# Divided weights in halves, shared by neighbouring products, 22 of their sums kept undivided, and a new order of 104 products

## The chip, the cores and the metric

One core of a Trainium2 chip runs the kernel. Its engines work through a queue each, in order: TensorE (PE, matmuls; PEld is its loading of weights), VectorE (DVE), ScalarE (ACT) and SyncE (SP, which here only issues transfers, DMAs). The metric is the device time of one execution in microseconds (us); lower is better.

## The reference

Sigmoid attention over 8 sequences of 448 tokens with 12 heads of 64, and on its output, 3584 tokens of 768 numbers, a two-layer network with 2048 hidden numbers. All inputs are float32, apart from the weights, which are float64.

```python
scores = scale * np.matmul(q, k.transpose(0, 1, 3, 2)) - np.log(S)
attn = 1.0 / (1.0 + np.exp(-scores))
x = np.matmul(attn, v)            # to (3584, 768)
h = x @ w_in                      # (768, 2048)
g = h * (1.0 / (1.0 + np.exp(-1.702 * h)))
out = g @ w_out                   # (2048, 768)
```

## The kernel before

**Attention** comes first on PE: all of its matmuls stand ahead of the first product of the network. Meanwhile the float64 weights are turned into 16 float32 pieces of 128x1536 (`decode`); the eight of `w_out` go to memory (`whole`, tiles `f`) and come back as `wf`.

**The two layers** are computed by a scheme in the manner of Strassen's. The tokens fall into two groups (q = 0, 1) of four blocks of 448; for each group and layer (m = 0, 1) there are 26 products instead of 32, so 2 x 2 x 26 = 104. A product is named (q, m, r). Its left operand is a sum of weight pieces (`W_SUMS`; the same value v for both groups), its right operand a sum of blocks of x (m = 0) or of g (m = 1), and sums of products (`H_SUMS`, `O_SUMS`) give h and the output. All these sums are DVE instructions (L784, L1218); results leave PSUM through ACT or DVE (L1184, L1185), or ACT puts a sum into PSUM ahead of a product that adds to it (L1142, L1144).

**Dividing.** Each operand of a product is divided into two numbers of the rounded type float32r: a cast gives the high part, a subtraction the rest. For weights that is `split_piece` (L803 on ACT or L804 on DVE, then L806 on DVE), for x and g it is `pair_of` (L1000/L1001, then L1012). A product is three matmuls for each of 12 pairs of blocks, 36 in all (L829).

**Where divided weights live.** `weights_ring` has two buffers (`raw64`) of 128x3072. The first time that a value (m, v) is wanted it is divided in such a buffer, and the divided piece is saved to memory at once (tile `c`, transfer `c<-w`). Each later time it is loaded (`w<-c`, 1536 KB). Nothing is kept from one product to the next, so product number i uses the buffer that product i - 2 leaves. `BUFS` sets how many buffers a kind has.

**Sums and memory.** Undivided sums lie in 14 slots of 128x1536 and 12 of 128x1792. `Sums.used` puts a value away if its next use is further off than `KEEP_FOR` says, in products: leaves of x, of the weights and spilled g are simply loaded again (`x<-xd`, `wf<-f`, `gl<-g`), others are written once (`kw`, `kx`, `kg`) and reloaded.

**The order.** `SEQUENCE` lists the 104 products by hand. `Plan.run` then steps through all tasks with a table of costs (`ISSUE`, `LANDING`, `PER_KB`, `act`, `dve`, `cast`) and puts each into its engine's queue in the order in which it would begin; where ACT and DVE can both do a task, it chooses. The program's queues are fixed by that.

Of the kernel before, what the change touches and what calls it, by code (L numbers as in the profile page):

```python
# [19 lines left out]
P = 128  # L20
# [9 lines left out]
    pair=2, q0=1, q1=1, q2=1, q3=1, h0=1, h1=1, z=1,  # L30
# [5 lines left out]
AGAIN = ((1, 0), (1, 1))  # L36
# [5 lines left out]
ISSUE, LANDING, PER_KB = 0.43, 2.2, 0.0027  # L42
# [72 lines left out]
class Plan:  # L115
    def __init__(self):
        self.tasks, self.rings, self.early, self.slotted, self.gate = [], {}, [], [], []

# [15 lines left out]
    def either(self, costs, emits, deps=(), uses=()):  # L134
        t = Task(emits, costs, deps)
        for b in dict.fromkeys(uses):
            b.users.append(t)
        self.tasks.append(t)
        return t

    def run(self, streams):
# [89 lines left out]
        while count < len(self.tasks):  # L231
# [36 lines left out]
            if e == "SP":  # L268
                free["SP"] = when + ISSUE
                free["DMA"] = max(free["DMA"], when) + cost * PER_KB  # L270
# [114 lines left out]
def sigmoid_attention_mlp(ctx: ExitStack, tc: tile.TileContext, qk, v, w, out):  # L385
# [415 lines left out]
    def split_piece(node, n, into, b, first=lambda: None):  # L801

        t_hi = on_either((act(n), lambda: nc.scalar.copy(into()[:, 0], node.view())),  # L803
                         (cast(n), lambda: nc.vector.tensor_copy(into()[:, 0], node.view())),  # L804
                         [*node.done], [b, node.b], first)
        t_lo = task("DVE", dve(n), lambda: nc.vector.tensor_tensor(  # L806
            into()[:, 1], node.view(), into()[:, 0].bitcast(F32), op=ALU.subtract), [t_hi], [b, node.b])
# [6 lines left out]
    def weights_ring(name):  # L814
        b = buffer("raw64")

        def first():
            if b.tile is None:
                make(b, "raw64", [P, 2 * PIECE], F32, name)

        return b, lambda: b.tile.bitcast(F32R).rearrange("p (t c) -> p t c", t=2), first
# [3 lines left out]
    def matmuls(ps, ws, x, todo, start, stop):  # L825

        for i, (c, k) in enumerate(todo):
            for j, (a, d) in enumerate(TERMS):
                nc.tensor.matmul(  # L829
                    ps, lhsT=ws[:, a, c * P : (c + 1) * P], rhs=x[:, d, k], start=start and i == 0 and j == 0,  # L830
                    stop=stop and i == len(todo) - 1 and j == 2, skip_group_check=True,
                )
# [13 lines left out]
    class Mlp:  # L846


        def __init__(self, sequence, before):
# [3 lines left out]
            self.w_later = {}  # L853
            self.saved, self.begun = {}, set()
# [8 lines left out]
            self.products_of = [(q, m, r) for q, m, r in sequence if q < 2]  # L863
            for i, (q, m, r) in enumerate(sequence):
                v = W_USES[r]
                if (m, v) not in self.begun:
                    self.begun.add((m, v))
                    self.w[m].need(v, i)
                if q < 2:
                    self.w_later[m, v] = self.w_later.get((m, v), 0) + 1  # L870
                    (self.x, self.g)[m][q].need((X_USES, G_USES)[m][r], i)
            self.begun.clear()
# [5 lines left out]
        def build(self):  # L878
            places = {}
            for now, (q, m, r) in enumerate(self.sequence):  # L880
                for sums in (*self.w, *self.x, *self.g):
                    sums.now = now
                if q == 2:
                    if (m, W_USES[r]) not in self.begun:
                        self.w_later[m, W_USES[r]] += 1
                        self.piece_of(q, m, r)
                    continue
# [75 lines left out]

        def piece_of(self, q, m, r):
            v = W_USES[r]
            self.w_later[m, v] -= 1
            self.begun.add((m, v))
            b, into, first = weights_ring(f"w{m}_{q}_{r}")
            if (m, v) in self.saved:
                t = dma(lambda: into().bitcast(F32), in_dram(m, v), 4 * KB, [self.saved[m, v]], [b], first)  # L970
            else:
                sums = self.w[m]
                node = sums.get(v)
                sums.left[v] -= W_USES.count(v)
                t = split_piece(node, PIECE, into, b, first)
                sums.used(v)
                if self.w_later[m, v]:
                    self.saved[m, v] = dma(in_dram(m, v), lambda: into().bitcast(F32), 4 * KB, [t], [b])
            return t, b, into
# [44 lines left out]
        def products(self, q, m, r, uses, n, parts, sign, onto, deps):  # L1024
# [4 lines left out]
            for i in range(parts):  # L1029
                todo = [(i * NJ + j, j) for j in range(NJ)] if m == 0 else [(c * NJ + i, c) for c in range(4)]  # L1030

                def emit(i=i, todo=todo):
                    if ps.tile is None:
                        make(ps, tag, [P, 4, 512], F32, f"p{m}_{q}_{r}")
                    matmuls(ps.tile[:, i, :T], weights(), xb.tile, todo, not more, True)

                t = task("PE", 3 * len(todo) * 0.2, emit, [t_x, t_w, *edge], [ps, xb, wb])
                self.units.append([t])
                done.append(t)
# [189 lines left out]
    last = {tag: plan.rings[tag][-1].users for tag in ("q0", "q1", "q2", "q3")}  # L1229
    mlp = Mlp(SEQUENCE, {"h0": [*last["q0"], *last["q1"]], "h1": [*last["q2"], *last["q3"]]})  # L1230
# [37 lines left out]
```

## Time and profile before

| | us |
|---|---|
| median of 3 runs | 1087.47 (1086.42 to 1089.45) |
| the profiled execution, device time | 1088.81 |
| its span, first to last instruction | 1087.0 |
| PE busy | 1033.0 (95%) |
| DVE busy | 942.3 (87%) |
| ACT busy | 564.6 (52%) |
| mean granted clock of PE | 0.992 |
| moved by DMA | 353.71 MB, 325 GB/s |

Times are of one profiled execution. "Idle before" in a row is the time for which the engine stood still ahead of those instructions, and the name behind the arrow is what ended it. Buffer numbers are left out of names: `w` is any divided weight piece (or a float64 piece in the attention stage), `p` a product in PSUM, `xp` and `gp` divided operands, `xs`, `gs`, `ws` sums, `h` and `o` sums of products.

### The profile page before, as it was taken

How to read it: one execution, taken by the hardware profiler on the slowest of the kernel's cores; microseconds unless marked ns; L12 is line 12 of the kernel's file. 1: busy time of each engine (PE TensorE's matmuls, PEld its weight loads, DVE VectorE, ACT ScalarE, POOL GpSimd, SP SyncE). 2: the span in 40 equal slices, each digit the busy share in tenths (PEclk: the TensorE clock that was granted, in tenths of full speed). 3: DMA queues.
4: the chain of work that ended last, by engine and by line, in shares of the span. 5: the costliest groups of instructions: out<-in, count | busy, mean ns of one | idle time of the engine just before them, and what ended most of it. 6: DMA issues, size and time to landing. Idle time of an engine off the chain costs nothing.

```text
span 1087.0 us, 13651 instructions
## 1 busy us (share of the span) xinstructions
PE 1033.0 (95%) x5588; PEld 836.8 (77%) x5588; DVE 942.3 (87%) x658; ACT 564.6 (52%) x452; POOL 0.2 (0%) x4
## 2 busy tenths in 40 slices
PE   9999999999999899798999989999999988999998
PEld 5554555557888789697888888889888877988887
DVE  6998899887998898898857987999999978879796
ACT  6888877774555665333533724654533422332243
POOL 0000000000000000000000000000000000000000
PEclk9999999999999999999999999999999999999999
DMA  8999888968898899969888976897977898888897
GB/s 336 378 351 389 317 313 323 332 240 319 357 375 330 298 380 347 348 222 355 299 286 322 368 309 249 320 403 280 345 300 292 319 353 346 337 342 316 300 349 268
DMA packets 57902, 353.71 MB, mean 325 GB/s; under 512 B 6000, under 2 KB 14320, under 8 KB 42480
## 3 DMA queue, kind: packets, MB, share of 16 engines
q1 hardware_dynamic: 57840, 352.84, 86.5%
q8 instruction: 44, 0.72, 0.3%
q14 instruction: 18, 0.15, 0.0%
HBM read 212.66 MB, written 140.15 MB: 325 GB/s over the span
## 4 chain that ended last, share of the span: by engine, by line
PE 65%; DMA 18%; DVE 11%; issue 4%; ACT 2%; SPq 0%; DVEq 0%; ACTq 0%
PE p L829 43%; DMA w<-c 13%; PE av L676 9%; PE sc L645 8%; DMA c<-w 3%; DVE h L1218 2%; DVE w L806 2%; PE sc L661 2%; DVE gp L1012 2%; PE av L689 2%; DVE xp L1012 1%; ACT h L1184 1%; DVE gs L784 1%; DMA kw<-ws 1%; DMA kw<-w 1%
## 5 line engine op out<-in xcount | busy, mean ns | idle before, releaser
L829 PE MATMUL p<-gp,w 128*128 128x448 f32 x1872 | 392.2, 370 | 26.6 <-DMA w<-c 17.4
L829 PE MATMUL p<-xp,w 128*128 128x448 f32 x1872 | 390.5, 369 | 22.9 <-DMA w<-c 13.6
L829 PEld LDWEIGHTS p<-gp,w 128*128 128x128 f32 x1872 | 353.3, 190 | 65.2 <-issue 23.7
L829 PEld LDWEIGHTS p<-xp,w 128*128 128x128 f32 x1872 | 352.1, 189 | 61.2 <-issue 21.4
L631 ACT ACTIVATE a<-sc,bias 128x896 f32<-128x896 f32 x168 | 155.9, 1015 | 46.8 <-PE sc L661 30.9
L1184 ACT COPY h<-p 128x1792 f32<-128x1792 f32 x38 | 62.7, 1657 | 107.3 <-PE p L829 78.2
L676 PE MATMUL av<-a,vraw 128*64 128x448 f32 x576 | 113.5, 543 | 0.0
L1184 ACT COPY o<-p 128x1344 f32<-128x1344 f32 x27 | 34.7, 1284 | 122.6 <-PE p L829 89.8
L645 PEld LDWEIGHTS sc<-qk 64*128 64x128 f32 x846 | 75.8, 184 | 26.5 <-PE sc L661 16.2
L645 PE MATMUL sc<-qk 64*128 64x448 f32 x846 | 94.2, 373 | 0.0
L1218 DVE TENSOR_TENSOR h<-h,p 128x1792 f32<-128x1792 f32 x39 | 77.7, 2018 | 13.2 <-ACT h L1184 9.0
L676 PEld LDWEIGHTS av<-a,vraw 128*64 128x64 f32 x576 | 39.2, 137 | 63.2 <-issue 45.1
L1045 ACT ACTIVATE h<-h 128x1792 f32<-128x1792 f32 x31 | 52.2, 1700 | 15.4 <-DVE h L1218 15.4
L515 DVE TENSOR_TENSOR qk<-qkraw,qk 128x896 fp32r<-128x896 f32 x47 | 50.6, 1088 | 0.6
L1000 ACT CAST gp<-gl 128x1792 fp32r<-128x1792 f32 x16 | 27.1, 1697 | 41.8 <-PE p L829 28.8
L1012 DVE TENSOR_TENSOR gp<-gl,gp 128x1792 fp32r<-128x1792 f32 x19 | 38.4, 2023 | 11.6 <-ACT gp L1000 11.5
L1218 DVE TENSOR_TENSOR h<-p,h 128x1792 f32<-128x1792 f32 x14 | 28.3, 2022 | 23.0 <-ACT h L1184 21.5
L1218 DVE TENSOR_TENSOR o<-o,p 128x1344 f32<-128x1344 f32 x27 | 41.6, 1550 | 5.0 <-PE p L829 5.0
L1012 DVE TENSOR_TENSOR xp<-x,xp 128x1344 fp32r<-128x1344 f32 x26 | 40.4, 1553 | 3.9 <-ACT xp L1000 3.9
L803 ACT CAST w<-ws 128x1536 fp32r<-128x1536 f32 x17 | 25.2, 1480 | 35.5 <-PE p L829 29.6
L1000 ACT CAST xp<-x 128x1344 fp32r<-128x1344 f32 x19 | 25.0, 1318 | 28.5 <-PE p L829 22.1
L806 DVE TENSOR_TENSOR w<-ws,w 128x1536 fp32r<-128x1536 f32 x22 | 38.6, 1753 | 1.2 <-ACT w L803 1.1
(113 smaller groups left out, 927.3 us busy)
## 6 DMA issues: line engine op xcount, KB each, us to landing
w<-c SPq DMA_DIRECT2D x56, 1536.0 KB, 7.7
c<-w SPq DMA_DIRECT2D x48, 1536.0 KB, 6.9
w<-w SPq DMA_DIRECT2D x16, 1536.0 KB, 10.0
qkraw<-qk SPq DMA_DIRECT2D x47, 448.0 KB, 6.7
gl<-g SPq DMA_DIRECT2D x20, 896.0 KB, 8.3
g<-h SPq DMA_DIRECT2D x16, 896.0 KB, 8.8
x<-xd SPq DMA_DIRECT2D x21, 672.0 KB, 8.8
kg<-kg SPq DMA_DIRECT2D x14, 896.0 KB, 8.3
```

The costliest lines, as they stand in the source:

```text
L515: lambda: nc.vector.tensor_tensor(lo(), src(), hi().bitcast(F32), op=ALU.subtract),
L631: nc.scalar.activation(a.tile, ps.tile[:, :, :S], AF.Sigmoid, bias=bias, scale=scale)
L645: nc.tensor.matmul(ps.tile[:, j, :S], lhsT=src[kk][rows, S + c * P : S + (c + 1) * P], rhs=src[qq][rows, :S], start=i == 0, stop=i == len( ...
L676: nc.tensor.matmul(ps.tile[cols, n % 2, :S], lhsT=vr.tile[:, at : at + D], rhs=a.tile[:, j], start=c == 0, stop=False, skip_group_check=True,)
L803: t_hi = on_either((act(n), lambda: nc.scalar.copy(into()[:, 0], node.view())), (cast(n), lambda: nc.vector.tensor_copy(into()[:, 0], node ...
L806: t_lo = task("DVE", dve(n), lambda: nc.vector.tensor_tensor(into()[:, 1], node.view(), into()[:, 0].bitcast(F32), op=ALU.subtract), [t_hi ...
L829: nc.tensor.matmul(ps, lhsT=ws[:, a, c * P : (c + 1) * P], rhs=x[:, d, k], start=start and i == 0 and j == 0, stop=stop and i == len(todo) ...
L1000: t_hi = on_either((act(n), lambda: nc.scalar.copy(part(0)(), node.view())), (cast(n), lambda: nc.vector.tensor_copy(part(0)(), node.view())),
L1012: nc.vector.tensor_tensor(part(1)(), node.view(), part(0)().bitcast(F32), op=ALU.subtract)
L1045: t = task("ACT", act(GB), lambda: nc.scalar.activation(view(), node.view(), AF.Gelu_apprx_sigmoid, scale=float(sign)), [*node.done, *(nod ...
L1184: t = on_either((act(self.n), lambda: nc.scalar.copy(view(), node.view())), (dve(self.n), lambda: nc.vector.tensor_copy(view(), node.view())),
L1218: nc.vector.tensor_tensor(view(), x.view(), y.view(), op=ALU.add if s0 == s else ALU.subtract)
```

## The change

Divided pieces are laid out in two halves, each with its high parts and its rests: half 0 serves the first six blocks of the piece, half 1 the others. The two buffers are now two tiles for the whole program, and each half is a buffer of its own for the order (`raw64` for half 0, `w1` for half 1), so that a load is two transfers of 768 KB; the second layer's products go through their blocks half by half. A product whose weights are still in one of the two buffers uses them as they are. `AGAIN` names 8 values of the first layer and 14 of the second that are never saved divided: their undivided sum is kept like any other, and they are divided for each use. `SEQUENCE` and `KEEP_FOR` have new numbers, and so have some costs of the planner.

In all, 56 products divide their weights (48 before), 31 share them (none before) and 17 load them (56 before); 14 divided pieces are saved (48 before).

```diff
-    pair=2, q0=1, q1=1, q2=1, q3=1, h0=1, h1=1, z=1,
+    pair=2, w1=2, q0=1, q1=1, q2=1, q3=1, h0=1, h1=1, z=1,
...
-AGAIN = ((1, 0), (1, 1))
...
-ISSUE, LANDING, PER_KB = 0.43, 2.2, 0.0027
+ISSUE, LANDING, PER_KB, MM = 0.43, (2.2, 2.5), 0.0027, 0.203
+PIECE_RATE = dict(load=0.0032, save=0.0027)
...
 SEQUENCE = (
-    (0, 0, 12), (0, 0, 18), (0, 0, 8), (0, 0, 17), (0, 0, 6), (0, 0, 9), (0, 0, 24), (0, 0, 25),
...
+    (0, 0, 17), (0, 0, 18), (0, 0, 24), (1, 0, 13), (0, 0, 13), (1, 0, 2), (0, 0, 2), (0, 0, 6),
...
+AGAIN = ((1, 5, 8, 11, 13, 17, 21, 24,), (1, 2, 4, 6, 8, 9, 10, 13, 15, 17, 18, 20, 21, 24,))
...
-    def split_piece(node, n, into, b, first=lambda: None):
+    def split_piece(node, n, into, b, wait):
+        def src():
+            return node.view().rearrange("p (h c) -> p h c", h=2)
-        t_hi = on_either((act(n), lambda: nc.scalar.copy(into()[:, 0], node.view())),
+        t_hi = on_either((act(n), lambda: nc.scalar.copy(into()[:, :, 0], src())),
...
     def in_dram(m, v):
-        return lambda: combined[m][v].rearrange("p (t c) -> p t c", t=2)
+        return lambda: combined[m][v].rearrange("p (h t c) -> p h t c", h=2, t=2)
...
+    def weights_ring():
+        old = plan.rings["raw64"][-2:]
+        a, b = buffer("raw64"), buffer("w1")
+        wait = [t for t in old[0].users] if len(plan.rings["w1"]) <= 2 else []
...
+        def into(part=None):
+            if a.turn not in ring_tiles:
+                make(a, "raw64", [P, 2 * PIECE], F32, f"w_{a.turn}")
+                ring_tiles[a.turn] = a.tile
+            at = ring_tiles[a.turn].bitcast(F32R).rearrange("p (h t c) -> p h t c", h=2, t=2)
+            return at if part is None else at[:, part]
+        return (a, b), into, wait
...
+        def ways(self):
+            ways, made, recent = [], set(), [None, None]
+            self.again = set()
+            for q, m, r in self.sequence:
+                v = W_USES[r]
+                if (m, v) in recent:
+                    ways.append("same")
+                    continue
+                if v in AGAIN[m] or (m, v) not in made:
+                    ways.append("made")
+                    made.add((m, v))
+                else:
+                    ways.append("loaded")
+                    self.again.add((m, v))
+                recent = [recent[1], (m, v)]
+            return ways
...
         def piece_of(self, q, m, r):
+            v, way = W_USES[r], self.way[self.now]
+            if way == "same":
+                return next(got for key, got in self.recent if key == (m, v))
+            b, into, wait = weights_ring()
+            if way == "loaded":
+                t = []
+                for h in range(2):
+                    t.append(dma(lambda h=h: into(h).bitcast(F32), lambda h=h: in_dram(m, v)()[:, h], 2 * KB,
+                                 [self.saved[m, v], *(wait if h else [])], [b[h]]))
+                    t[h].rate = PIECE_RATE["load"]
             else:
                 sums = self.w[m]
                 node = sums.get(v)
-                sums.left[v] -= W_USES.count(v)
+                sums.left[v] -= 1
+                t = [split_piece(node, PIECE, into, b, wait)] * 2
                 sums.used(v)
-                if self.w_later[m, v]:
+                if (m, v) in self.again:
+                    save = dma(in_dram(m, v), lambda: into().bitcast(F32), 4 * KB, t[:1], b)
...
-            for i in range(parts):
-                todo = [(i * NJ + j, j) for j in range(NJ)] if m == 0 else [(c * NJ + i, c) for c in range(4)]
+            if m == 0:
+                units = [(i, i // 2, [(i * NJ + j, j) for j in range(NJ)], True, True) for i in range(parts)]
+            else:
+                units = [(i, h, [(c * NJ + i, c) for c in (2 * h, 2 * h + 1)], h == 0, h == 1) for h in range(2) for i in range(parts)]
```

What this does to the queues shows at two places. The first is PE's queue, at the program's last products; `w1_0_8` and the like are divided weights (before: one tile for each use; now `w_0` and `w_1` throughout), `DMAHW...` among the waits stands for a transfer. Before:

```order
L829 MATMUL p1_0_25_7585<-gp0_10_7565,w1_0_25_7567 128x448 [waits DVE_49,DMAHW4_49,PE_49,Activation_49]
L829 MATMUL p1_0_25_7585<-gp0_10_7565,w1_0_25_7567 128x448 x35
L829 MATMUL p1_0_5_7636<-gp0_23_7617,w1_0_5_7615 128x448 [waits DVE_49,DMAHW6_49,PE_49,Activation_49]
L829 MATMUL p1_0_5_7636<-gp0_23_7617,w1_0_5_7615 128x448 x35
L829 MATMUL p1_0_8_7671<-gp0_29_7666,w1_0_8_7668 128x448 [waits DVE_49,DMAHW1_49,PE_49,Activation_49]
L829 MATMUL p1_0_8_7671<-gp0_29_7666,w1_0_8_7668 128x448 x35
```

PE's queue at the same place now:

```order
L845 MATMUL p1_1_6_7631<-gp1_33_7622,w_1_2493 128x448 [waits DVE_49,PE_49,Activation_49]
L845 MATMUL p1_1_6_7631<-gp1_33_7622,w_1_2493 128x448 x35
L845 MATMUL p1_0_6_7683<-gp0_33_7674,w_1_2493 128x448 [waits DVE_49,Activation_49]
L845 MATMUL p1_0_6_7683<-gp0_33_7674,w_1_2493 128x448 x35
L845 MATMUL p1_1_0_7739<-gp1_42_7715,w_0_2647 128x448 [waits DVE_49,PE_49,Activation_49]
L845 MATMUL p1_1_0_7739<-gp1_42_7715,w_0_2647 128x448 x35
```

Before, each of these products waits for a transfer of its own weights; now none does, and the first two use the same piece.

The second place is SP's queue near the 35th product, where divided weights are loaded in both programs (`w<-c`). Before:

```order
L483 DMA w0_1_0_4510<-c0_9_120 128x3072
L483 DMA g0_5_198<-h0_28_3915 128x1792
L483 DMA w0_1_15_4557<-c0_12_123 128x3072
L483 DMA kg1_10_220<-h1_10_3559 128x1792
L483 DMA w0_1_19_4607<-c0_20_131 128x3072
L483 DMA kg1_12_222<-h1_26_4350 128x1792
L483 DMA w0_1_23_4644<-c0_23_134 128x3072
```

SP's queue at the same place now:

```order
L487 DMA w_1_2493<-c0_2_114 128x1536 x2
L487 DMA w_0_2647<-c0_15_126 128x1536
L487 DMA kw0_10_2_4475<-kw0_10_217 128x1536
L487 DMA kx0_16_1_4477<-kx0_16_229 128x1344
L487 DMA w_0_2647<-c0_15_126 128x1536
L487 DMA kw0_15_1_4524<-kw0_15_218 128x1536
L487 DMA w_1_2493<-c0_22_133 128x1536 x2
L487 DMA kx0_15_1_4571<-kx0_15_219 128x1344
```

Each load is two rows of half the size, and between them stand reloads of undivided sums of weights (`kw`) and of x (`kx`), of which there were none at this place.

More of the change, by code (lines that the diff above doesn't have):

```diff
@@ new lines @@
+    w1={0: 12, 1: 12, 2: 3, 3: 6, 4: 25, 5: 12, 6: 6, 8: 12, 9: 12, 10: 25, 11: 3, 13: 25, 15: 3, 17: 12, 18: 25, 19: 6, 20: 3, 21: 3, 22: 6, 23: 3, 24: 3, 25: 6},
+    x0={0: 12, 1: 3, 2: 6, 3: 3, 4: 3, 5: 25, 7: 3, 8: 25, 9: 3, 10: 12, 12: 6, 13: 6, 14: 12, 15: 6, 16: 12, 17: 3, 20: 3, 23: 25, 24: 3},
+    x1={0: 25, 1: 3, 2: 12, 3: 6, 5: 6, 6: 6, 7: 6, 8: 12, 10: 25, 11: 25, 12: 12, 13: 6, 14: 25, 15: 12, 16: 12, 17: 6, 18: 3, 19: 6, 20: 6, 21: 12, 22: 3, 24: 6, 25: 3},
+    g0={0: 12, 1: 25, 2: 12, 4: 12, 5: 25, 6: 12, 8: 6, 9: 12, 10: 3, 11: 3, 12: 3, 13: 12, 14: 6, 15: 25, 16: 25, 17: 3, 18: 12, 20: 3, 21: 12, 22: 6, 23: 6, 24: 3, 25: 25, 26: 25, 29: 3, 30: 6, 31: 3, 32: 25, 35: 12, 37: 6, 38: 6, 39: 12, 40: 25, 41: 6, 42: 25},
@@ L117, in __init__ @@
         self.tasks, self.rings, self.early, self.slotted, self.gate = [], {}, [], [], []
+        self.landing = LANDING[0]
     def buffer(self, tag):
@@ L135, in either @@
         t = Task(emits, costs, deps)
+        t.landing = self.landing
         for b in dict.fromkeys(uses):
@@ L269, in run @@
                 free["SP"] = when + ISSUE
-                free["DMA"] = max(free["DMA"], when) + cost * PER_KB
+                free["DMA"] = max(free["DMA"], when) + cost * t.rate
                 end = free["DMA"] + t.landing
@@ L799, in tiled @@
         return flat if n == PIECE else lambda: flat().rearrange("p (a b) -> p a b", b=T)
-    def split_piece(node, n, into, b, first=lambda: None):
-        t_hi = on_either((act(n), lambda: nc.scalar.copy(into()[:, 0], node.view())),
-                         (cast(n), lambda: nc.vector.tensor_copy(into()[:, 0], node.view())),
-                         [*node.done], [b, node.b], first)
+    def split_piece(node, n, into, b, wait):
+        def src():
+            return node.view().rearrange("p (h c) -> p h c", h=2)
+        t_hi = on_either((act(n), lambda: nc.scalar.copy(into()[:, :, 0], src())),
+                         (cast(n), lambda: nc.vector.tensor_copy(into()[:, :, 0], src())),
+                         [*node.done, *wait], [*b, node.b])
         t_lo = task("DVE", dve(n), lambda: nc.vector.tensor_tensor(
-            into()[:, 1], node.view(), into()[:, 0].bitcast(F32), op=ALU.subtract), [t_hi], [b, node.b])
+            into()[:, :, 1], src(), into()[:, :, 0].bitcast(F32), op=ALU.subtract), [t_hi], [*b, node.b])
         node.readers += [t_hi, t_lo]
@@ L811, in in_dram @@
     def in_dram(m, v):
-        return lambda: combined[m][v].rearrange("p (t c) -> p t c", t=2)
[L814 to L821, printed above, removed]
+        return lambda: combined[m][v].rearrange("p (h t c) -> p h t c", h=2, t=2)
+    ring_tiles = {}
+    def weights_ring():
+        old = plan.rings["raw64"][-2:]
+        a, b = buffer("raw64"), buffer("w1")
+        wait = [t for t in old[0].users] if len(plan.rings["w1"]) <= 2 else []
+        half = PIECE // 2
+        def into(part=None):
[5 more added lines that the diff above has]
+        return (a, b), into, wait
     gate = plan.gate
@@ L829, in matmuls @@
                 nc.tensor.matmul(
-                    ps, lhsT=ws[:, a, c * P : (c + 1) * P], rhs=x[:, d, k], start=start and i == 0 and j == 0,
+                    ps, lhsT=ws(c // 6)[:, a, c % 6 * P : (c % 6 + 1) * P], rhs=x[:, d, k], start=start and i == 0 and j == 0,
                     stop=stop and i == len(todo) - 1 and j == 2, skip_group_check=True,
@@ L852, in __init__ @@
                            KEEP_FOR[f"w{m}"], self.put_w(m)) for m in range(2)]
-            self.w_later = {}
-            self.saved, self.begun = {}, set()
+            self.saved, self.recent = {}, [(None, None)]
+            self.way = self.ways()
             self.x = [Sums(X_SUMS[0], X_USES, self.x_leaf(q), dve(XB), combine, fresh(f"xs{q}", XB, "s"),
@@ L863, in __init__ @@
             self.products_of = [(q, m, r) for q, m, r in sequence if q < 2]
+            for m in range(2):
+                for v in W_USES:
+                    self.w[m].left[v] -= 1
             for i, (q, m, r) in enumerate(sequence):
[L865 to L868, printed above, removed]
+                if self.way[i] == "made":
+                    self.w[m].left[W_USES[r]] += 1
+                    self.w[m].need(W_USES[r], i)
                 if q < 2:
-                    self.w_later[m, v] = self.w_later.get((m, v), 0) + 1
                     (self.x, self.g)[m][q].need((X_USES, G_USES)[m][r], i)
-            self.begun.clear()
             for q in range(2):
@@ L882, in build @@
                     sums.now = now
+                self.now = now
                 if q == 2:
-                    if (m, W_USES[r]) not in self.begun:
-                        self.w_later[m, W_USES[r]] += 1
-                        self.piece_of(q, m, r)
+                    self.piece_of(q, m, r)
                     continue
@@ L962, in put_g @@
             return put
-        def piece_of(self, q, m, r):
[L965 to L970, printed above, removed]
+        def ways(self):
[14 more added lines that the diff above has]
+            return ways
+        def piece_of(self, q, m, r):
+            v, way = W_USES[r], self.way[self.now]
[8 more added lines that the diff above has]
+                    t[h].rate = PIECE_RATE["load"]
             else:
@@ L973, in piece_of @@
                 node = sums.get(v)
-                sums.left[v] -= W_USES.count(v)
-                t = split_piece(node, PIECE, into, b, first)
+                sums.left[v] -= 1
+                t = [split_piece(node, PIECE, into, b, wait)] * 2
                 sums.used(v)
-                if self.w_later[m, v]:
-                    self.saved[m, v] = dma(in_dram(m, v), lambda: into().bitcast(F32), 4 * KB, [t], [b])
+                if (m, v) in self.again:
+                    save = dma(in_dram(m, v), lambda: into().bitcast(F32), 4 * KB, t[:1], b)
+                    save.rate = PIECE_RATE["save"]
+                    self.saved[m, v] = save
+            self.recent = [self.recent[-1], ((m, v), (t, b, into))]
             return t, b, into
@@ L1028, in products, with emit @@
             edge = [*(self.before[tag] if len(plan.rings[tag]) == 1 else []), *deps]
-            for i in range(parts):
-                todo = [(i * NJ + j, j) for j in range(NJ)] if m == 0 else [(c * NJ + i, c) for c in range(4)]
-                def emit(i=i, todo=todo):
+            if m == 0:
+                units = [(i, i // 2, [(i * NJ + j, j) for j in range(NJ)], True, True) for i in range(parts)]
+            else:
+                units = [(i, h, [(c * NJ + i, c) for c in (2 * h, 2 * h + 1)], h == 0, h == 1) for h in range(2) for i in range(parts)]
+            for i, h, todo, first, last in units:
+                def emit(i=i, todo=todo, first=first, last=last):
                     if ps.tile is None:
                         make(ps, tag, [P, 4, 512], F32, f"p{m}_{q}_{r}")
-                    matmuls(ps.tile[:, i, :T], weights(), xb.tile, todo, not more, True)
-                t = task("PE", 3 * len(todo) * 0.2, emit, [t_x, t_w, *edge], [ps, xb, wb])
+                    matmuls(ps.tile[:, i, :T], weights, xb.tile, todo, first and not more, last)
+                t = task("PE", 3 * len(todo) * MM, emit, [t_x, t_w[h], *edge], [ps, xb, wb[h]])
                 self.units.append([t])
-                done.append(t)
+                if last:
+                    done.append(t)
             return done
@@ L1229, in sigmoid_attention_mlp @@
     last = {tag: plan.rings[tag][-1].users for tag in ("q0", "q1", "q2", "q3")}
+    plan.landing = LANDING[1]
     mlp = Mlp(SEQUENCE, {"h0": [*last["q0"], *last["q1"]], "h1": [*last["q2"], *last["q3"]]})
```

10 lines of the change are left out of this document (3 added, 7 removed), and 24 rows, old and new, of the table SEQUENCE.

## The prediction

> **What bounds the kernel now.** The page's totals come first, then the chain that ended last: the work of TensorE (PE) and waits for transfers make up most of it.
>
> ```profile
> span 1087.0 us, 13651 instructions
> PE 1033.0 (95%) x5588; PEld 836.8 (77%) x5588; DVE 942.3 (87%) x658; ACT 564.6 (52%) x452; POOL 0.2 (0%) x4
> PE 65%; DMA 18%; DVE 11%; issue 4%; ACT 2%; SPq 0%; DVEq 0%; ACTq 0%
> PE p L829 43%; DMA w<-c 13%; PE av L676 9%; PE sc L645 8%; DMA c<-w 3%; DVE h L1218 2%; DVE w L806 2%; PE sc L661 2%; DVE gp L1012 2%; PE av L689 2%; DVE xp L1012 1%; ACT h L1184 1%; DVE gs L784 1%; DMA kw<-ws 1%; DMA kw<-w 1%
> ```
>
> The order of instructions puts all of attention on PE ahead of the first product, so the second view is the windows of the two stages (columns: window, its length, busy us of PE, PEld, DVE, ACT, POOL with instructions, granted clock, DMA share, GB/s).
>
> ```profile
> 0.00:252.50 252.50, 251.10 (x1844) 131.45 (x1845) 217.84 (x226) 199.07 (x203) 0.20 (x4) 1.00 0.89 328
> 252.50:1084.00 831.50, 781.86 (x3744) 705.31 (x3744) 724.43 (x432) 365.39 (x250) 0.00 (x0) 0.99 0.87 326
> ```
>
> Attention leaves PE 1.4 us idle, and PE's order there does not change: I keep its 252.5 us. The stage of the 104 products takes 831.1 us, to the end of the last matmul below (1083.6). PE idles 49.5 us in it (26.6 + 22.9 in the page's two groups of products); the view of PE's waits in this stage says for what, and PE's timeline shows places.
>
> ```profile
> PE p L829 <- DMA w<-c: 31.0, 21, 4.7
> PE p L829 <- DVE gp L1012: 6.1, 6, 1.6
> PE p L829 <- DVE xp L1012: 5.1, 7, 1.5
> PE p L829 <- DVE w L806: 2.4, 2, 1.3
> ```
>
> ```profile
> 252.51 14.83 PE L829 MATMUL p<-xp,w 128*128 128x448 f32 x72 [0.23 <-DVE xp L1012]
> 370.50 8.06 PE L829 MATMUL p<-xp,w 128*128 128x448 f32 x37 [0.38 <-DMA w<-c]
> 453.01 38.28 PE L829 MATMUL p<-xp,w 128*128 128x448 f32 x180 [4.44 <-DMA w<-c]
> 558.22 30.97 PE L829 MATMUL p<-xp,w 128*128 128x448 f32 x144 [2.12 <-DMA w<-c]
> 716.02 59.34 PE L829 MATMUL p<-gp,w 128*128 128x448 f32 x288 [1.06 <-DVE gp L1012]
> ```
>
> And the end of the timeline of all engines:
>
> ```profile
> 1066.97 0.32 SPq L483 DMA_DIRECT2D w<-c  x1
> 1069.92 2.02 DVE L1012 TENSOR_TENSOR gp<-gl,gp 128x1792 fp32r<-128x1792 f32 x1
> 1075.92 7.67 PE L829 MATMUL p<-gp,w 128*128 128x448 f32 x36 [1.54 <-DMA w<-c]
> ```
>
> Three readings. One product is 36 matmuls, and eight in a row without a wait took 59.34 us: 7.42 us each. Second, 31.0 of the 49.5 idle us, in 21 waits, are for divided weights that come back from memory. The last three rows show how: the load is issued at 1066.97, when the product before the last ended and freed its buffer; only one product lies between, and the load lands 8.9 us later, 1.54 us after that product is done. Third, nothing else was late there: the other operand was ready at 1069.92 + 2.02 = 1071.94, four microseconds before. So this time is PE's to win, until VectorE (DVE), 87% busy in the stage, is late in its turn.
>
> A fourth reading is the clock (third column from the end):
>
> ```profile
> 450.00:500.00 50.00, 46.44 (x220) 42.41 (x221) 42.37 (x29) 17.74 (x13) 0.00 (x0) 0.97 0.77 281
> 900.00:950.00 50.00, 46.48 (x218) 42.05 (x219) 44.30 (x27) 15.77 (x11) 0.00 (x0) 0.97 0.89 351
> ```
>
> ```profile
> 453.00:456.00 3.00, 2.99 (x8) 2.69 (x9) 3.00 (x3) 0.99 (x1) 0.00 (x0) 0.52 1.05 442
> 509.40:512.00 2.60, 2.56 (x13) 2.42 (x14) 2.10 (x2) 0.49 (x1) 0.00 (x0) 1.00 1.07 378
> 558.20:561.00 2.80, 2.78 (x9) 2.55 (x10) 0.39 (x1) 0.00 (x0) 0.00 (x0) 0.63 1.02 345
> ```
>
> Cut into stretches of 50 us, the stage has five at 0.97 (the first and the last are shown) and the rest at 1.00. In each a wait for weights is followed by some 3 us at about half clock, as at 453 and 558. 0.03 x 50 x 5 = 7.5 us go there, counted as busy. Check of the model: 104 x 7.42 + 49.5 + 7.5 = 828.7 of 831.1; the 2.4 left are ends of broken stretches.
>
> **The change, part by part.** The transfers and the groups of instructions give the prices (mean or median in each row).
>
> ```profile
> w<-c SPq DMA_DIRECT2D x56, 1536.0 KB, 7.7
> c<-w SPq DMA_DIRECT2D x48, 1536.0 KB, 6.9
> gl<-g SPq DMA_DIRECT2D x20, 896.0 KB, 8.3
> x<-xd SPq DMA_DIRECT2D x21, 672.0 KB, 8.8
> kg<-kg SPq DMA_DIRECT2D x14, 896.0 KB, 8.3
> kw<-kw SPq DMA_DIRECT2D x11, 768.0 KB, 8.2
> wf<-f SPq DMA_DIRECT2D x11, 768.0 KB, 11.7
> kx<-kx SPq DMA_DIRECT2D x5, 672.0 KB, 9.3
> ```
>
> ```profile
> L806 DVE TENSOR_TENSOR w<-ws,w 128x1536 fp32r<-128x1536 f32 x22 | 38.6, 1753 | 1.2 <-ACT w L803 1.1
> L803 ACT CAST w<-ws 128x1536 fp32r<-128x1536 f32 x17 | 25.2, 1480 | 35.5 <-PE p L829 29.6 <-DVE ws L784 3.3 <-DMA c<-w 2.6
> L804 DVE CAST w<-ws 128x1536 fp32r<-128x1536 f32 x5 | 4.8, 958 | 0.2 <-DMA c<-w 0.2
> L1218 DVE TENSOR_TENSOR o<-o,p 128x1344 f32<-128x1344 f32 x27 | 41.6, 1550 | 5.0 <-PE p L829 5.0
> L1185 DVE COPY o<-p 128x1344 f32<-128x1344 f32 x7 | 10.9, 1556 | 10.2 <-ACT o L1184 5.7 <-PE p L829 4.3
> L1184 ACT COPY o<-p 128x1344 f32<-128x1344 f32 x27 | 34.7, 1284 | 122.6 <-PE p L829 89.8 <-DVE o L1218 14.4 <-DMA out<-o 10.4
> ```
>
> DVE's waits for transfers in the stage, the two longest of three:
>
> ```profile
> DVE xs L784 <- DMA kw<-w: 4.9, 1, 4.9
> DVE x L784 <- DMA x<-xd: 0.5, 1, 0.5
> ```
>
> *Weights.* Of the 104 products 56 now divide their weights afresh (48 before), 31 use those of a neighbour, and 17 load (56 before). So the wait that cost 31.0 us meets 17 loads instead of 56. Each is two halves, and a half is issued when the product two weights earlier has finished with that half: half a product, 3.7 us, more head start, 11.1 us against the 7.7 of a whole load. Bounds: 0 if that hides all, 17 x 31.0/56 = 9.4 if a load waits as long as now. I take 2, near the hidden end, since 8.9 us (the example above) fits into 11.1. The matmuls are as many in both programs; those of the second layer now run half by half, at no cost I can see.
>
> *Clock.* The dips follow the long waits, so four of five should go: 6.0 us, between 0 and 7.5. The Trainium skill, "TensorE: Matmul & The Clock Gate", Part 1, says that the array falls to half clock after at least one idle window of about 3.4 us. This trace agrees only in part: 0.63 was granted after a gap of 2.12 us. By the page only the gaps over 3.4 us, the 4.44 us at 453 and one of 4.7, would matter, two of the five, and the sum would come out 3.0 us higher.
>
> *Dividing on ACT and DVE.* Eight more divisions: 8 x 1.753 on DVE and five more casts on ACT (5 x 1.48 = 7.4), three on DVE (2.9). The pieces are now written as 2 x 768 with a stride; no row shows a DVE cast of that form. Between 0.958 and the slow pass of 1.753, 12 casts, that is 0 to 9.5 us of DVE; I take 0, since the runs of 768 are still contiguous. Counting all other instructions of both orders, DVE loses 8 sums of 1344 (12.4) and 8 copies out of PSUM (12.9), and gains 0.8 in small ones: 16.9 - 12.4 - 12.9 + 0.8 = -7.6 us. ACT gains 13 copies of 1344 (16.7), loses 8 of 1792, and fills PSUM ahead of 40 products instead of 28 (about 15): some 25 us, on an engine that is busy for 365 of 831 us; nothing of it is on the path.
>
> *How evenly DVE is loaded.* I add up DVE's instructions between the starts of products, by their rows. The work exceeds 7.42 us a product by 9 us over the worst run before (21 products, which hold the 59.34 us without a wait), by 7 us over the worst run now (one product). So the waits that aren't for weights should stay what they are: 49.5 - 31.0 = 18.5 us, DVE's for the most part. A faster PE leaves less slack, a smaller DVE load gives some back; I leave it at 18.5.
>
> *Transfers.* 39 loads and 34 saves of 1536 KB go (-114.8 MB). To free memory the new table sends sums away sooner: 147 reloads of x, g and w operands instead of 82, and 51 writes instead of 26 (+71.7 MB). In all -43 MB of the stage's 271 (326 GB/s x 831.5 us), which at 800 us is 285 GB/s. DVE waited for transfers of such operands hardly more than 5 us in this stage before, at its very start. I cost the 65 added reloads at nothing; the cover is that they are issued products ahead. If it goes, each is a trip of 8 to 12 us. The queue of SyncE issues some thirty more transfers at 0.32 us, 10 us over 800.
>
> *The end* stays: 1087.0 - 1083.6 = 3.4 us.
>
> **Sum:** 252.5 + 104 x 7.42 (771.7) + 18.5 + 2 + 1.5 (one dip) + 1.5 (ends of stretches) + 3.4 = 1051.1 us of span. The profiled execution took 1088.81 for its 1087.0, and the median of the runs, 1087.47, is 1.3 below it: 1051.1 + 1.8 - 1.3 = 1051.6. I say 1051.
>
> **Rivals.** *DVE is the bound.* From 252.51 to 370.1 nothing waited for weights, and 15 products still took 117.6 us, 7.84 each, with small waits for DVE. If that is the pace everywhere: 252.5 + 815.4 + 3.4 + 0.5 = 1072. For it: DVE would be busy for 717 of 800 us. Against it: the 59.34 us.
>
> *Everything hides.* The DVE waits shrink too: 252.5 + 771.7 + about 8 + 3.4 + 0.5 = 1036. The smaller, evener DVE load speaks for it, the waits of 1.0 to 1.6 us for DVE all over the stage against it.
>
> *Late reloads, slower than before.* DVE takes its queue in order; if a reload isn't there, every later sum and division waits, and PE runs dry. Four or five lost trips of 8.3 us eat the 36 us; from there on it is slower, and eight give about 1051 + 66 = 1117. The 65 added reloads, and their place on one SyncE queue behind loads that wait for PE, speak for it; against it speak 5 us of such waits in 82 reloads, and a lower DMA load.
>
> *No change:* DVE is late by as much wherever weights were late, 1087. The four microseconds of slack in the rows at 1069.92 speak against it.
>
> **Chances and range.** My forecast (1040 to 1064) 0.62, DVE's pace (1064 to 1078) 0.15, everything hides (1030 to 1040) 0.10, no change 0.05, late reloads 0.08. The range from 1034 to 1077 leaves out the last two, and the ends of the two before. A measurement of this kernel tells 0.3% from no change: faster 0.87, same 0.05, slower 0.08.
>
> **What would show it.** Right: PE's waits for `w<-c` at a few us; product stretches of 7.42 each; no stretch at half clock after the start; DVE busy above 89% of the stage; the first product still near 252.5. Wrong: a row of DVE waiting for `kg`, `kw`, `kx`, `x` or `wf` with more than 15 us in total (late reloads), PE waiting for `w` or `gp` divisions for over 35 us (DVE's pace), casts of 2x768 at 1.7 us, or a long wait at the first product of the second layer, which now stands 27th instead of 45th.

## The result, and the profile after

| | before | after |
|---|---|---|
| median | 1086.95 us | 1042.84 us (1038.97 to 1045.04) |
| profiled execution, device time | 1088.81 us | 1043.49 us |
| its span | 1087.0 us | 1041.7 us |
| PE idle in the products' stage | 49.5 us | 11.7 us |
| moved by DMA | 353.71 MB | 310.63 MB |

The ratio is 0.9587, with a 95% interval of 0.9554 to 0.9621: 4.1% faster. The forecast was 1051 us, range 1034 to 1077.

The page of the changed kernel: totals, and the chain that ended last.

```profile
span 1041.7 us, 13721 instructions
PE 1024.7 (98%) x5588; PEld 832.3 (80%) x5588; DVE 933.7 (90%) x654; ACT 588.4 (56%) x473; POOL 0.2 (0%) x4
PE 34%; DVE 3%; issue 0%; DMA 0%; ACT 0%; DVEq 0%; ACTq 0%
PE p L845 34%; DVE gp L1052 1%; DVE o L1262 1%; DVE w L813 0%; DVE kg L788 0%; DMA wf<-f 0%; DVE h L1262 0%; DVE wf L788 0%; ACT p L1186 0%; DVE xp L1052 0%; ACT o L1228 0%; DVE gp L1041 0%; ACT o L1116 0%; DVEq L788 0%; ACTq L1186 0%
```

This chain is followed back only to 640 us, so its shares cannot be set beside those of before; from there on it is almost only matmuls, and `w<-c`, 13% of the chain before, is not in it. The two stages (columns as before), PE's waits in the second, and four rows of PE's timeline:

```profile
0.00:253.00 253.00, 251.15 (x1840) 131.42 (x1844) 217.23 (x225) 201.41 (x204) 0.20 (x4) 1.00 0.90 334
253.00:1040.00 787.00, 773.56 (x3752) 700.84 (x3744) 716.52 (x429) 387.03 (x269) 0.00 (x0) 1.00 0.76 287
```

```profile
PE p L845 <- DVE xp L1052: 7.5, 10, 1.7
PE p L845 <- ACT p L1186: 1.9, 2, 1.5
PE p L845 <- DVE w L813: 1.1, 1, 1.1
PE p L845 <- PE p L845: 0.6, 1, 0.6
PE p L845 <- DVE gp L1052: 0.2, 1, 0.2
PE p L845 <- DVE xp L1054: 0.2, 1, 0.2
```

```profile
253.67 14.86 PE L845 MATMUL p<-xp,w 128*128 128x448 f32 x72
650.98 22.14 PE L845 MATMUL p<-xp,w 128*128 128x448 f32 x108 [1.46 <-ACT p L1186]
672.96 320.38 PE L845 MATMUL p<-gp,w 128*128 128x448 f32 x1548
993.56 44.76 PE L845 MATMUL p<-gp,w 128*128 128x448 f32 x216 [0.22 <-DVE gp L1052]
```

No wait for a weight load is left, the granted clock is 1.00 in both stages, and from 672.96 on 43 products run without a gap: 320.38 / 43 = 7.45 us each. Nearly all that PE still waits for is VectorE or ScalarE, mostly in the first layer. The transfers that correspond to those of before:

```profile
w<-c SPq DMA_DIRECT2D x34, 768.0 KB, 5.8
kg<-kg SPq DMA_DIRECT2D x27, 896.0 KB, 7.4
gl<-g SPq DMA_DIRECT2D x26, 896.0 KB, 7.4
x<-xd SPq DMA_DIRECT2D x34, 672.0 KB, 7.4
c<-w SPq DMA_DIRECT2D x14, 1536.0 KB, 8.0
kw<-kw SPq DMA_DIRECT2D x25, 768.0 KB, 7.4
```

The reloads became more and land sooner (7.4 us where they took 8.2 to 8.8), at 287 GB/s instead of 326; the 14 saves `c<-w` land later (8.0 us instead of 6.9).

### The profile page after: what moved, and what is told of

The parts are those of the page before. It is cut to its first block, busy times and chain, and to the rows that moved or that the text cites. A ratio compares the mean times of both kernels' runs of the same rounds, so it can differ in the third digit from the quotient of the medians.

```text
span 1041.7 us, 13721 instructions
## 1 busy us (share of the span) xinstructions
PE 1024.7 (98%) x5588; PEld 832.3 (80%) x5588; DVE 933.7 (90%) x654; ACT 588.4 (56%) x473; POOL 0.2 (0%) x4
## 2 busy tenths in 40 slices
DMA packets 62799, 310.63 MB, mean 298 GB/s; under 512 B 6544, under 2 KB 14864, under 8 KB 58896
## 5 line engine op out<-in xcount | busy, mean ns | idle before, releaser
L1228 ACT COPY h<-p 128x1792 f32<-128x1792 f32 x30 | 49.7, 1657 | 106.7 <-PE p L845 65.0
L1228 ACT COPY o<-p 128x1344 f32<-128x1344 f32 x37 | 47.1, 1283 | 101.8 <-PE p L845 95.5
L1262 DVE TENSOR_TENSOR o<-o,p 128x1344 f32<-128x1344 f32 x34 | 52.2, 1549 | 7.5 <-ACT o L1228 5.1
L1089 ACT ACTIVATE h<-h 128x1792 f32<-128x1792 f32 x28 | 47.5, 1702 | 14.5 <-DVE h L1262 14.5
L710 DVE COPY x<-av 128x896 f32<-128x896 f32 x23 | 25.1, 1089 | 18.6 <-PE av L693 18.6
L1052 DVE TENSOR_TENSOR gp<-gs,gp 128x1792 fp32r<-128x1792 f32 x19 | 38.4, 2022 | 2.6 <-ACT gp L1040 2.2
L1052 DVE TENSOR_TENSOR gp<-kg,gp 128x1792 fp32r<-128x1792 f32 x18 | 36.3, 2019 | 1.7 <-ACT gp L1040 1.5
L813 DVE TENSOR_TENSOR w<-ws,w 128x1536 fp32r<-128x1536 f32 x19 | 33.3, 1752 | 1.3 <-ACT w L810 1.1
L514 DVE CAST qk<-qkraw 128x896 fp32r<-128x896 f32 x37 | 22.8, 622 | 12.4 <-DMA qkraw<-qk 6.1
L813 DVE TENSOR_TENSOR w<-kw,w 128x1536 fp32r<-128x1536 f32 x18 | 31.5, 1752 | 2.6 <-ACT w L810 2.6
```

What stands on the lines that cost most here:

```text
L514: (costs[1], lambda: nc.vector.tensor_copy(hi(), src())),
L710: (1.09, lambda: nc.vector.tensor_copy(xb.tile, ps.tile[:, :, :S])), [t], [xb, ps], rows)
L813: t_lo = task("DVE", dve(n), lambda: nc.vector.tensor_tensor(into()[:, :, 1], src(), into()[:, :, 0].bitcast(F32), op=ALU.subtract), [t_hi ...
L1052: nc.vector.tensor_tensor(part(1)(), node.view(), part(0)().bitcast(F32), op=ALU.subtract)
L1089: t = task("ACT", act(GB), lambda: nc.scalar.activation(view(), node.view(), AF.Gelu_apprx_sigmoid, scale=float(sign)), [*node.done, *(nod ...
L1228: t = on_either((act(self.n), lambda: nc.scalar.copy(view(), node.view())), (dve(self.n), lambda: nc.vector.tensor_copy(view(), node.view())),
```

## The experiments

Every kernel here is ordered anew by the planner inside it, so an edit also moves instructions that it doesn't name. How much that alone can do is the last group's question. "PE idle" is that of the products' stage, from the view of PE's waits. Each ratio is to runs of the kernel before that were made beside it, whose medians lie between 1086.95 and 1088.86.

| | median us | ratio to before (95%) | PE idle | of it weight loads | DMA MB |
|---|---|---|---|---|---|
| before | 1086.95 | 1 | 49 | 31.0 | 353.71 |
| after | 1042.84 | 0.9587 (0.9554 to 0.9621) | 11.5 | 0 | 310.63 |
| 1 old order, halves | 1092.09 | 1.0034 (1.0016 to 1.0052) | 49 | 1.9 | 347.43 |
| 2 old order, whole loads | 1102.37 | 1.0124 (1.0102 to 1.0146) | 55 | 21.1 | 347.41 |
| 3 new order, nothing shared | 1211.93 | 1.1121 (1.1093 to 1.1149) | 141 | 126.5 | 420.73 |
| 4 after, whole loads | 1055.41 | 0.9689 (0.9669 to 0.971) | 22 | 11.1 | 310.62 |
| 5 as 1, old costs | 1100.15 | 1.0125 (1.0093 to 1.0157) | 54 | 1.5 | 347.43 |
| 6 as 1, own queue | 1093.09 | 1.0059 (1.004 to 1.0078) | 50 | 9.0 | 347.43 |
| 7 after, no sum kept | 1056.70 | 0.9731 (0.9697 to 0.9766) | 23 | 0 | 331.07 |
| 8 after, old costs | 1054.36 | 0.9698 (0.9657 to 0.974) | 23 | 0 | 310.63 |
| 9 after, divided for each | 1098.76 | 1.0116 (1.0087 to 1.0145) | 56 | 0 | 315.34 |
| 10 after, saves back | 1103.66 | 1.0151 (1.0135 to 1.0167) | 61 | 3.5 | 376.69 |
| 11 after, casts on ACT | 1051.37 | 0.9668 (0.9652 to 0.9685) | 21 | 0 | 310.63 |
| 12 after, matmul cost | 1049.51 | 0.9654 (0.9639 to 0.9668) | 18 | 1.0 | 310.63 |

**Are the weight loads the whole story?** Experiment 1 takes the waits for them away and keeps the old order.

```diff
 SEQUENCE = (
-    (0, 0, 17), (0, 0, 18), (0, 0, 24), (1, 0, 13), (0, 0, 13), (1, 0, 2), (0, 0, 2), (0, 0, 6),
+    (0, 0, 12), (0, 0, 18), (0, 0, 8), (0, 0, 17), (0, 0, 6), (0, 0, 9), (0, 0, 24), (0, 0, 25),
...
-AGAIN = ((1, 5, 8, 11, 13, 17, 21, 24,), (1, 2, 4, 6, 8, 9, 10, 13, 15, 17, 18, 20, 21, 24,))
+AGAIN = ((), ())
```

(`KEEP_FOR` as before, too.)

> The changed kernel with the old order of products, the old table of what is put away, and no sum kept undivided: 54 of 104 products load their weights, in halves, 2 share. Theory 1 (what was won is the lateness of divided weights; a head start is enough): each load gets 3.7 us of head start, of the 31.0 us of waits for weights only what exceeds 3.7 us stays (two waits, about 2 us), and the half-clock dips go: 1087 - 29 - 7 = about 1051. Theory 2 (the new order with its evener VectorE work wins the time): the order is the old one, so 1080 to 1087. Rival 3 (transfers are limited by bandwidth, with the same bytes as before): loads land as late as now, 1080 or more.

PE's waits in the products' stage (us in total, times, longest):

```profile
PE p L845 <- issue: 13.2, 4, 6.8
PE p L845 <- DVE gp L1052: 9.2, 7, 2.3
PE p L845 <- DVE xp L1052: 8.5, 10, 1.4
PE p L845 <- DVE w L813: 5.9, 5, 1.3
PE p L845 <- ACT h L1228: 3.7, 1, 3.7
...
PE p L845 <- DMA w<-c: 1.9, 2, 1.5
```

Half of theory 1 holds: in halves, the waits for loads fall from 31.0 to 1.9 us, as expected. The other half falls: nothing is won, 1092, above theory 2's range too, and rival 3's late loads are not in the rows. As much idle time is there as before, 49 us, under other names. The longest of the waits called "issue" shows whose they are (timeline of the same run):

```profile
789.90 3.98 PE L845 MATMUL p<-gp,w 128*128 128x448 f32 x18 [0.42 <-DMA w<-c]
794.64 2.03 DVE L788 TENSOR_TENSOR h<-h,gs 128x1792 f32<-128x1792 f32 x1
796.76 1.68 ACT L1040 CAST gp<-h 128x1792 fp32r<-128x1792 f32 x1 [1.57 <-DVE h L788]
798.52 2.02 DVE L1052 TENSOR_TENSOR gp<-h,gp 128x1792 fp32r<-128x1792 f32 x1
800.64 5.57 PE L845 MATMUL p<-gp,w 128*128 128x448 f32 x18 [6.77 <-issue]
```

PE is done at 793.9; the last sum for its next operand starts at 794.64 and the division ends at 800.54, a tenth of a microsecond before PE goes on. By the timeline DVE has had no break since 785.8; it came to this operand only now. In the kernel before, the same operand was ready hardly earlier, at 800.31:

```profile
798.28 2.03 DVE L1012 TENSOR_TENSOR gp<-h,gp 128x1792 fp32r<-128x1792 f32 x1
```

There PE had waited 2.63 us for weights at 794.39 and went on from that product to this one without a gap. At this place the weights' lateness had covered the lateness of the operand. The last product, on which the prediction's third reading rests, is another case. Its operand was ready at 1071.94 in the kernel before and is ready at 1076.98 here:

```profile
1074.95 2.03 DVE L1052 TENSOR_TENSOR gp<-gl,gp 128x1792 fp32r<-128x1792 f32 x1
1077.07 3.46 PE L845 MATMUL p<-gp,w 128*128 128x448 f32 x9 [3.43 <-issue]
```

Two sums of g now stand close ahead of its division in DVE's queue (from 1068.37 and 1071.77), and PE waits 3.43 us for it. So a part of the new idle time comes from the planner's new placing; how much, these runs do not say.

Experiment 2 undoes the halves in that kernel: one transfer, `[self.saved[m, v], *wait], b)` for both halves.

> As the first, but each load is one transfer of 1536 KB, which waits until both halves of the buffer are free: the kernel before, with the new cost table of the planner and two products that share. Theory 1: about 1085, with waits for weights of about 30 us. Theory 2: the same. If the planner's costs alone had won the time, about 1045.

1102, where I had expected about 1085. It is 10 us slower than the first, with 21.1 us of waits for loads. So in the old order halves take 19 us of waits away and are worth 10 us, but 1102 is 15 us above the kernel before, from which it differs by the planner's costs, the layout in halves and two shared products. Experiment 5 puts the costs back with halves:

```diff
-ISSUE, LANDING, PER_KB, MM = 0.43, (2.2, 2.5), 0.0027, 0.203
-PIECE_RATE = dict(load=0.0032, save=0.0027)
+ISSUE, LANDING, PER_KB, MM = 0.43, (2.2, 2.2), 0.0027, 0.2
+PIECE_RATE = dict(load=0.0027, save=0.0027)
```

> As the first experiment (old order, loads in halves, no sum kept), but with the planner's old costs, so that only the halves and two shared products differ from the kernel before. Theory 1 (a head start for the weights is enough; in the first experiment the new costs spoiled an order that was tuned with the old ones): 1055. Theory 4, from the first experiment (in the old order VectorE's divisions and reloads are late right behind the weights, whatever the costs): waits for weights of 2 us again, but 1075 to 1090.

1100, slower than both expectations, again with hardly a wait for loads (1.5 us). So nothing shows that the new costs held experiment 1 back. The next suspect is SyncE's queue, on which reloads stand behind loads that wait for PE; experiment 6 issues the loads from GpSimd's queue (`nc.gpsimd.dma_start` for `w<-c` alone):

> As the first experiment, but the loads of divided weights are issued from GpSimd's queue instead of SyncE's. Theory 4a (in the old order the reloads of operands stand behind weight loads that wait for PE on SyncE's queue, and this head-of-line wait makes VectorE late): the waits for divisions shrink, about 1060. Theory 4b (the order itself, the distance between a sum and its use, makes VectorE late): 1085 to 1095, as the first.

1093, as the first: theory 4a finds no support. It is not refuted either, since this queue is no like for like: GpSimd is then 58.6 us busy with issuing, and 9.0 us of waits for loads come back.

**What the new order needs.** Experiment 3 gives the kernel before the new `SEQUENCE` and `KEEP_FOR` and nothing else.

> The kernel before with the new order and the new table of what is put away: 48 products divide and save, 56 load whole pieces, none share. Theory 1: a neighbour now loads what was saved a product before; a save (6.9 us) and a load (7.7 us) in a row against 7.4 us of cover cost some 4 us for about 27 such pairs, so slower than before: 1130 to 1200, with all of it in waits for weights. Theory 2 (the order as such wins): 1050 to 1065.

The longest of PE's waits:

```profile
PE p L829 <- DMA w<-c: 126.5, 33, 9.1
```

1212: a neighbour that can't share has to wait for a save and a load. There are 33 such waits at 3.8 us, where I had expected some 27 at 4; the time lies above the expected 1130 to 1200. PE idles 92 us more than before, and the rest of the 125 us goes with a lower granted clock (0.946 instead of 0.992). The new order does not pay without sharing. Experiment 4 takes the halves from the changed kernel's 17 loads, with the same edit as experiment 2:

> The changed kernel with its 17 loads in one transfer each instead of two halves. Theory 1 as predicted (17 loads that cost 31.0/56 us each if they are as late as before): up to 9 us of waits for weights come back and a dip or two, 1045 to 1056. Rival: sharing and few loads hide them without halves: 1043, no wait for weights.

The two longest of PE's waits:

```profile
PE p L845 <- DMA w<-c: 11.1, 6, 4.0
PE p L845 <- DVE xp L1049: 7.5, 9, 1.6
```

The 12.6 us that it loses are nearly all in one row: 11.1 us in six waits for whole loads, while the waits for xp stay where they were (7.5). In this order, what halves win arrives in the time.

Experiment 9 keeps the order and lets nobody share, dividing the 31 pieces again:

```diff
-                if (m, v) in recent:
-                    ways.append("same")
-                    continue
-                if v in AGAIN[m] or (m, v) not in made:
+                if (m, v) in recent or v in AGAIN[m] or (m, v) not in made:
```

> The changed kernel in which no product uses a neighbour's weights: the 31 shared pieces are divided again for each product (87 divisions, 17 loads, same order of products). VectorE gets 31 x 1.753 = 54 us more and is wanted for about 771 of the 785 us that the products' stage takes. Theory 4b (VectorE is what the order has to keep ahead; sharing spares it): 1070 to 1100, with the loss in waits for divisions of w, xp and gp. If VectorE's load leaves room: 1045 to 1055.

The four longest of PE's waits:

```profile
PE p L845 <- DVE gp L1049: 22.4, 17, 2.9
PE p L845 <- ACT p L1183: 11.5, 3, 10.3
PE p L845 <- DVE xp L1049: 9.2, 8, 2.1
PE p L845 <- DVE w L813: 7.9, 9, 1.3
```

The stage's window in the same run (DVE is the fifth number):

```profile
253.00:1100.00 847.00, 790.36 (x3748) 711.63 (x3744) 772.98 (x465) 423.92 (x296) 0.00 (x0) 0.98 0.73 272
```

1099, within theory 4b's 1070 to 1100. DVE now works 773 us in the stage, 56 more, and most of what PE waits for is divisions. That the time grows by 56 as well is partly chance: 10.3 us are one wait for ScalarE to fill PSUM, at the product where experiments 8 and 11 below lose as much, and the granted clock is 0.98. Sharing is what leaves DVE the room in which the weights' waits can be cashed in.

Experiment 7 keeps no sum undivided (`AGAIN = ((), ())`), with the new order and sharing.

> The changed kernel with no value kept as an undivided sum: 48 divisions, 24 or 25 loads in halves, 31 shared, 22 pieces saved. Its memory traffic for saves and loads of divided pieces grows by some 8 of each. Theory 1: the loads are hidden by halves and sharing, so the kept sums are worth little: 1043 to 1050. Rival (the kept sums are what frees the time): 1060 or more, with waits for weights.

1057: between the two expectations. There is no wait for loads, as theory 1 has it; the 12 us of added idle time are waits for divisions. Keeping the sums comes out as 14 us here, and the last group shows that placing alone can make 7 to 12 us.

**The transfers.** Experiment 10 saves every divided piece again (`if True:` for `if (m, v) in self.again:`), 42 writes that nobody reads.

> The changed kernel that also saves each of the 56 freshly divided pieces to memory; nothing more reads them (42 writes of 1536 KB, 66 MB, so about as much traffic as the kernel before). Rival 3 (the smaller traffic wins the time): 1065 or more, with later loads and reloads. Theories 1 and 4: the buffer is also held until the save has read it, but neighbours share, so little: 1043 to 1052.

The two longest of PE's waits, and the stage's window:

```profile
PE p L845 <- DVE gp L1052: 22.7, 11, 4.3
PE p L845 <- ACT h L1228: 18.1, 1, 18.1
```

```profile
253.00:1100.00 847.00, 785.13 (x3744) 710.95 (x3744) 726.57 (x438) 374.87 (x260) 0.00 (x0) 0.97 0.89 342
```

1104, all of the gain and more. I had expected 1043 to 1052; the rival's 1065 or more is right, though at 377 MB this kernel moves 23 MB more than the one before. Reloads land later (`x` after 9.4 us and `kg` after 8.7, where both took 7.4). But PE waits for hardly any transfer itself (3.5 us), and DVE's waits for transfers in the stage are 6.0 us, where they were 4.7 (ACT's 13.4, where they were 1.7). One wait of 18.1 us for a copy out of PSUM and many for gp make up the most. Behind the 18.1 us the timeline shows no transfer: the copy stands on ACT behind a gelu, which waits for a sum on DVE, and DVE works without a break from 513.1 to 528.5:

```profile
526.45 2.02 DVE L1262 TENSOR_TENSOR h<-h,h 128x1792 f32<-128x1792 f32 x1
528.50 1.70 ACT L1089 ACTIVATE h<-h 128x1792 f32<-128x1792 f32 x1 [10.77 <-DVE h L1262]
530.11 3.19 ACT L1228 COPY h<-p 128x1792 f32<-128x1792 f32 x2
```

The planner counts these writes too, and places the rest around them. At this place it is the order of work on ACT and DVE; whether the chip's transfers or the planner's placing does the rest, these runs don't separate.

**How much is placing?** Three small edits of the changed kernel: the old costs (8, the diff of experiment 5), all 56 weight casts on ACT (11), and `MM` 0.206 for 0.203 (12).

> The changed kernel with the planner's old costs (landing, rate, matmul); the list of products is the same, so instructions only move a few places in their queues. If the order of products does the work: 1040 to 1050. If the fit between the list and the planner's costs does it: 1055 or more, with the loss in waits for VectorE's divisions.

> The changed kernel with every weight cast on ScalarE (56 instead of 44), 12 x 0.96 = 11.5 us less for VectorE and 12 x 1.48 more for ScalarE, which is half idle. If VectorE's load sets the remaining 12 us of PE waits: 1036 to 1041. If their places in the queues do: 1040 to 1050.

> The changed kernel with the planner's cost of a matmul at 0.206 us, which is what the trace has for long stretches (320.38 us for 1548), instead of 0.203; instructions move a few places. If the fit of the planner's costs to the chip matters most: 1036 to 1041. If the list was fitted to the costs as they are: 1045 to 1055.

All three are slower than the changed kernel, by 7 to 12 us. Experiment 12 is in its second range; 8 lies between its two, and its loss is not in divisions but in one wait for ScalarE. Experiment 11 is slower than both expectations: DVE has only 2 us less work (714 us in the stage instead of 717) where 11.5 were expected, since the planner gave it other tasks. In 8 and 11 it is one place (PE's timelines):

```profile
658.52 24.98 PE L845 MATMUL p<-xp,w 128*128 128x448 f32 x108 [10.35 <-ACT p L1186]
```

```profile
659.48 24.64 PE L843 MATMUL p<-xp,w 128*128 128x448 f32 x108 [10.07 <-ACT p L1184]
```

In the changed kernel the same three products start at 650.98 after a wait of 1.46 us for the same instruction, ScalarE filling PSUM ahead of them. In experiment 8 the timeline has it on ACT behind gelus and copies that take turns with sums and copies on DVE, each waiting for the other's last. So differences of about 10 us between two placings of one list say nothing on the edit, unless a row shows them, as in experiment 4.

## Why the prediction was right, point by point

- *The sum.* Forecast 1051.1 us of span, measured 1041.7. The stage before took 253.7 instead of 252.5; 104 products at 7.42 with ends of stretches 773.2, measured 784.65 - 11.7 = 773.0; the end 3.4, as said. Small changes of the planner's costs move this kernel by 7 to 12 us, so an agreement within 9.4 us is partly luck.
- *Weight loads:* 2 us, measured 0. Experiment 4 shows the halves as the cause: with whole loads 11.1 us come back, a little above the bound of 9.4. A half has a head start and a shorter trip; no run takes the two apart.
- *Clock:* 1.5 us for one dip left, measured none. The longest gap is now 1.7 us; the shortest gap that a dip followed was 2.12 us in the kernel before and 1.79 us in experiment 6.
- *The term that was mis-sized* is the waits that aren't for weights: 18.5 us, measured 11.7. That is 6.8 of the 9.4 us; the loads and the dip make up 3.5, and the attention stage takes 1.2 back. "A faster PE leaves less slack, a smaller DVE load gives some back" was left at zero; the waits shrank, but no run shows that the smaller load did it. The 11.7 us are nearer to the rival in which everything hides (about 8) than to the forecast.
- *DVE and ACT:* -7.6 us on DVE, measured 942.3 - 933.7 = 8.6 less, 7.9 of it in the stage; some 25 more on ACT, measured 588.4 - 564.6 = 23.8. The cast in the form 2 x 768 costs what it did (0 of the 0 to 9.5 us; the group's row, which writes the form as 128x1536):

```profile
L811 DVE CAST w<-ws 128x1536 fp32r<-128x1536 f32 x5 | 4.8, 955 | 0.1
```

The Trainium skill, "VectorE: DVE Perf Modes", "What auto-detection actually checks", says that the double rate of this kind is taken if a single source and the destination are in SBUF with outermost non-unit dimensions that are both even or equal. The row of 955 ns agrees; no run here breaks the condition.

- *Late reloads:* costed at nothing, measured 4.7 us of DVE's waits for transfers in the stage, with 147 reloads. The longest is for a write (`kx<-xs`); the reloads themselves make up 1.9 us. The cover held; the three longest:

```profile
DVE ws L788 <- DMA kx<-xs: 2.0, 1, 2.0
DVE ws L788 <- DMA wf<-f: 1.0, 1, 1.0
DVE gs L788 <- DMA gl<-g: 0.9, 1, 0.9
```

- *What the prediction got for the wrong reason.* It took the 31.0 us as PE's to win, because the other operand lay ready four microseconds before at the place shown. In the old order that does not come true: experiment 1 has hardly a wait for weights and the same PE idle time, and at that very place the operand came 3.43 us late. Beside experiment 2, which has the same costs and layout, it wins 10 us for 19 us of waits. The rival "no change", with a chance of 0.05, is what the halves measured in the old order, with the placing moved too. The prediction weighed the evenness of DVE's work in the new order, but only for the other waits. The 31 us are won in the new order, and not without sharing (experiment 9), which has the operands ready as well. Experiment 10 loses the gain with the saves back, and which part of that is transfers stays open.

## What to carry to other kernels

A wait in PE's list is what came last, not what would be won: before a gain is put on it, look at more than one place for what comes next, or take the wait away alone on the chip. Here static queues couple two engines that are busy for 90% and more of the time, and taking away the waits of one alone won nothing over the kernel before. The list that was fitted to a planner's costs lost 0.6 to 1.1% in each of three small edits. Sharing an operand between neighbours paid twice here: no load, and no second division, had to be done for it.

## What the runs showed of the hardware

Half-clock stretches followed a gap of 2.12 us in the kernel before and one of 1.79 us in experiment 6 (granted clock 0.57 over the next 2.6 us). None followed a gap of 2.49 us in the kernel before, nor one of 3.43 us in experiment 3 (1.00 over the next 2.6 us). Between 1.8 and 3.4 us the length of a gap alone does not decide in these rows. A load of 768 KB landed in 5.8 us (median) where one of 1536 KB took 7.5 (experiment 4), so halving a transfer saved far less than half of its trip. By an estimate from these numbers, the earlier start of a half (half a product of 7.4 us) is worth more than its shorter trip (1.7 us); no run takes the two apart. The kernel with 42 unread writes more, placed anew, was 61 us slower, at 342 GB/s instead of 287 in the stage, with only 3.5 us of PE's waits for loads.
